# A planned attention and feed-forward kernel: load estimates, mask products, priorities and the last output re-laid

## The chip, the core and the metric

The kernel runs on one NeuronCore of a Trainium2 chip. The metric is the device time of one execution in microseconds (us), lower being better. A core has a matrix engine (TensorE, "PE"), whose products go to PSUM banks; a vector engine (VectorE, "DVE") and a scalar engine (ScalarE, "ACT"), which read PSUM and SBUF; GpSimd ("POOL"), which copies within SBUF and here issues the loads; and SyncE ("SP"), which here issues stores and transposing transfers. Each engine runs its own instructions in order and waits on semaphores for the others.

## The reference

Eight batches of eight heads with 576 tokens and 64 columns go through masked attention; the result is laid out as 4608 tokens of 512 columns and goes through a feed-forward block with a squared relu.

```python
scores = scale * np.matmul(q, k.transpose(0, 1, 3, 2))
mask_local = (rel >= 0) & (rel < stride)                    # stride = 32, heads 0 to 3
mask_strided = (rel >= 0) & (pos[None, :] % stride == pos[:, None] % stride)   # heads 4 to 7
scores = np.where(masks[None, :, :, :], scores, -1000000000.0)
attn = np.exp(scores - np.max(scores, axis=-1, keepdims=True))
attn = attn / (np.sum(attn, axis=-1, keepdims=True) + 1e-09)
x = np.matmul(attn, v)            # then transposed to (4608, 512)
h = x @ w_in                      # (512, 2048)
r = np.maximum(h, 0.0)
g = s * (r * r) + b
out = g @ w_out                   # (2048, 512)
```

## The kernel before

**Attention.** Heads are handled in pairs, four pairs to a batch, called (b, m). Pairs m = 0 and 1 are local: six tiles of 96 queries against 128 keys. Pairs 2 and 3 are strided: eight tiles of 72. A pair (`pair_steps`) transposes q and k, either on PE (`trans`) or from batch 3 to 5 on by a transposing transfer on SP (`k_dma`, `q_dma`); spreads q so that its two heads lie in separate columns (`q_spread`, a copy on ACT, DVE or POOL); forms scores (`score`, L623); takes exponentials on ACT (L641); multiplies by v with a column of ones for the sums (`av`, L684); divides on DVE; and transposes the result into `xT`, on PE or by a transfer. In batch 0 (`b < PE_MASK`) the mask is added in PSUM: each score product of 192 or 144 columns is preceded by a product of the identity with large negative numbers (L620). From batch 1 on the mask is a multiplication on DVE after the exponential.

**Feed-forward.** The 4608 tokens are nine tiles T of 512. `ff1` (L983) multiplies `xT` by `w_in`, ACT or DVE take the relu and the square. T = 0 and 1 go through `ff2` (L1238). From T = 2 on the second product uses seven products P1 to P7 of halves instead of eight (`ff2_seven`, L951), and T = 7 and 8 do the same for the first one (`ff1_seven`, L1208). In the last tile P3 comes last; its 16 products go to two banks, eight for rows t = 0 and eight for t = 1, and each bank is evicted by one `scalar_tensor_tensor` on DVE into a tile "o" and stored by SP (`store`, L882 and L886). The tiles "o" come from a pool of three buffers (`op`), taken in turn; a new one waits until the store of the third one before it has landed.

**The order.** Nothing is ordered by hand on the engines. `lay_out` runs a planner (`class Plan`) in the host's Python that keeps an assumed time `t` of PE and emits, one after another, the steps of attention and feed-forward in the order that all engines then run. PE steps are chosen in the loop at the end: attention if it is behind its due time (`due`, with the constant `ahead`), otherwise feed-forward. Work for the other engines is posted with what it needs and its assumed cost (`post`), and `flush` emits what is ready, the smallest ready time plus a priority first. Priorities by kind of work stand in `ORDER`. `ORDERS` is 0, so the order is taken as it stands.

When data of a load will be there is assumed too: `landing(cost)` keeps a time `ring` at which the stream of loads is through, adds the cost of each load, and adds 0.6 us, or 6 us after 60 us. Transposing transfers ("D", "Y") count as landed 12 us, copies out to DRAM ("X") 7 us after their issue (`LAT`). The loads of batch b + 2 (`fetch_qk`, then `fetch_v`) are posted to POOL when batch b's q and k are through and the k transfers of batch b + 1 are under way; in front of them stand two small copies on POOL (`gate`, L1323) which wait for these transfers. After v has landed, `rows_before` copies its rows by 32 partitions, on ACT or DVE, queued at the planned time of the landing.

At the start PE runs filler products (`keep_running`, L1502) until q and k are there.

Of the kernel before, what the change touches and what calls it, by code (L numbers as in the profile page):

```python
# [18 lines left out]
class Plan:  # L19
# [7 lines left out]
    LAT = {"A": 70.0, "V": 70.0, "P": 70.0, "D": 12000.0, "X": 7000.0, "Y": 12000.0}  # L27

    def __init__(self, order):
        self.t = 0.0  # L30
        self.SLACK, self.ahead, self.LATER = order["SLACK"], order["ahead"], order
        self.done = {}
        self.pend = []
        self.free = {"A": 0.0, "V": 0.0, "P": 7000.0, "D": 0.0, "X": 0.0, "Y": 0.0}
        self.banks = {}

# [7 lines left out]

    def flush(self):
        while True:
            best = None
            for p in self.pend:
                r = self.ready_at(p[0])
                if r is None or r > self.t:  # L50
                    continue
                if p[1].keys() <= {"A", "V"} and min(
                        self.free[e] for e in p[1]) > self.t + self.SLACK:
                    continue
                k = p[3][0]
                w = r + self.LATER.get(k[0] if isinstance(k, tuple) and k[2:3] != (0,) else None, 0.0)
                if best is None or w < best[0]:
                    best = (w, r, p)
            if best is None:
                return  # L60
            _, r, p = best
            self.pend.remove(p)
            eng = min(p[1], key=lambda e: max(self.free[e], r) + p[1][e])
            end = max(self.free[eng], r, self.t - self.SLACK) + p[1][eng]
            self.free[eng] = end
            p[2](eng)
            for k in p[3]:
                if isinstance(k, Group):
                    self.banks[k.name] = end + self.LAT[eng]
                    k = ("rel", k)  # L70
                soon = isinstance(k, tuple) and k[0] == "soon"
                self.done[k] = end + (6000.0 if soon else p[4] or self.LAT[eng])

# [44 lines left out]
class Step:  # L118
    def __init__(self, fn, ns, needs=(), group=None, keys=(), posts=(), after=None):
# [4 lines left out]
ORDER = {"g": 1500.0, "S": 2500.0, "in": 2500.0, "w_mix": 0.0, "wc": 1000.0, "ev": 1000.0,  # L124
         "c21": 1500.0, "c11": 500.0, "c12": 500.0, "C22": -1500.0, "fv": 0.0, "Vb": -400.0,
         "x": -1500.0, "Ub": 1000.0, "xc": -1500.0, "fe": -400.0, "k": 1500.0, "fu": -1500.0,
         "Va": 500.0, "p": 0.0, "c22": 500.0, "Ua": 2500.0, "e": -1500.0, "q": 0.0, "r": 0.0,
         "u": 0.0, "SLACK": 600.0, "ahead": 0.05}
KINDS = ("g", "S", "in", "w_mix", "wc", "Va", "Ua", "Ub", "Vb", "C22", "xc", "q", "k", "r", "x", "e",
         "p", "u", "ev", "fv", "fu", "fe", "c11", "c22", "c21", "c12")  # L130


def varied(order, rnd):

    order = dict(order)
    for kind in rnd.sample(KINDS, rnd.choice((1, 2, 4))):
        order[kind] = rnd.choice((-1500.0, -800.0, -400.0, 0.0, 500.0, 1000.0, 1500.0, 2500.0))
    if rnd.random() < 0.2:
        order["SLACK"] = rnd.choice((400.0, 600.0, 800.0, 1000.0))
    if rnd.random() < 0.2:  # L140
        order["ahead"] = rnd.choice((0.0, 0.05, 0.1, 0.2))
    return order
# [46 lines left out]
def lay_out(ctx, tc, nc, q, k, v, moe_w_in, moe_w_out, moe_s, moe_b, out, order, q_shape, out_shape,  # L189
# [284 lines left out]
    def pair_steps(b, m):  # L474
# [135 lines left out]
        def score(i, group):  # L610
# [3 lines left out]
            def f():  # L614
                if i % per_s == 0:
                    st["s", g] = bank(group)
                c = i % per_s * 2 * nq
                if b < PE_MASK:

                    nc.tensor.matmul(  # L620
                        out=st["s", g][0:nk, c:c + 2 * nq], lhsT=ident[0:nk, 0:nk],
                        rhs=neg_loc if loc else neg_str, start=True, stop=False)
                nc.tensor.matmul(  # L623
                    out=st["s", g][0:nk, c:c + 2 * nq], lhsT=(st["k"][:, i * nq:i * nq + nk] if loc else st["k"][:, i, 0:SQ]),
                    rhs=st["q"][:, i].rearrange("d e c -> d (e c)"), start=b >= PE_MASK, stop=True)

            s = Step(f, (2 if b < PE_MASK else 1) * (2 * nq / 2.4 + 8), needs=[("q", id_), ("k", id_)],
                     group=group if i % per_s == 0 else None)
# [30 lines left out]

        gr = None  # L660
        for i in range(nt):
            if i % per_s == 0:
                gr = group_of("s", b, m)
            steps.append(score(i, gr))
# [188 lines left out]
    def ff2_seven(T):  # L853
# [24 lines left out]
        def store(i, k, of, plus, ts=slice(0, 2)):  # L878
            def g(eng):
# [3 lines left out]
                    out=o[:, ts], in0=src, scalar=s_sb[:, 0:1],  # L883
                    in1=plus()[:, ts], op0=ALU.mult, op1=ALU.add)
# [3 lines left out]
                        "(t p) m -> p t m", p=128)[:, ts], in_=o[:, ts])  # L888
# [51 lines left out]
        for key, group, name, fresh, lhs, rhs, needs, more, posts in seq:  # L940
            for t in range(2):
                for k in range(H):
                    halves = last and name == "W"

                    def f(k=k, t=t, group=group, name=name, fresh=fresh, lhs=lhs, rhs=rhs, key=key,
# [3 lines left out]
                        elif fresh and t == k == 0:  # L949
                            gts[name, T] = bank(group).rearrange("p (t m) -> p t m", t=2)  # L950
                        nc.tensor.matmul(out=gts[name, T, t][:, 0] if halves else gts[name, T][:, t],  # L951
                                         lhsT=lhs(k, t), rhs=rhs(k),
                                         start=fresh and k == 0 and (halves or t == 0),
                                         stop=t == 1 and k == H - 1, skip_group_check=True)
                    s = Step(f, 110, needs=needs(k) + ([(x[0], T, t) if halves and x == d("C22")
# [3 lines left out]
                    if k == H - 1 and key == "P3" and last:  # L959
                        s.keys = [("P3", T, t)]  # L960
                        s.posts = [([("P3", T, t)], {"V": 420.0},
                                    store(0, 1, "W", val("Ub"), slice(t, t + 1)),
                                    [Ws[t]])]
# [3 lines left out]
                    if t == 1 and k == H - 1 and key == "P3":  # L967
# [338 lines left out]
    ring = 0.0  # L1306
    LONG_V = 4

    def landing(cost):

        nonlocal ring
        ring = max(ring, plan.t + 2000.0) + cost

        return ring + (6000.0 if plan.t > 60000.0 else 600.0)
# [4 lines left out]
    def fetch_qk(b):  # L1319
# [6 lines left out]
        for name in ("q", "k"):  # L1326
            if b >= (QB_DMA if name == "q" else KB_DMA):
                arrive(both(name + "l", b), landing(4600))
                continue
            if b < HEAD_T:  # L1330
                arrive(both(name + "l", b), landing(2400 if name == "q" else 2600))
                continue
            plan.done["raw", name, b] = landing(1700 if b > 1 else 2400 if name == "q" else 2500)
            for mm in range(2):
                pair_post(b, name, mm, ("raw", name, b))
        for name in ("qs", "ks"):
            arrive(both(name, b), landing(2000 if b > 1 else 1200))

    def fetch_v(b):
        load_vl(b)  # L1340
        plan.done["raw", "vl", b] = landing(4600)
# [4 lines left out]
        else:  # L1346
            load_vs(b)
            arrive(both("vs", b), landing(5000))

    def early_v(b):  # L1350
# [3 lines left out]
        plan.done["raw", "v", False, b] = landing(1800 if b > 1 else 1300)  # L1354
# [27 lines left out]
    plan.done["sb_row",] = 16000.0  # L1382
    def weights_in(eng):

        nonlocal ring
        nc.gpsimd.tensor_copy(out=gate[0:8, 2:3], in_=loaded[0, "qs"][64:SQ, 0:1])
        load_w_in()
        ring = 13200.0
        for keys, cost in ([0], 2700), ([1], 2500), ([2], 2500), ([3], 2500):
            arrive([("w_in", c) for c in keys], landing(cost))  # L1390
# [7 lines left out]
    def weights_out(chunks):  # L1398
        load_w_out(chunks)
        for c in chunks:  # L1400
            arrive([("w_out", c)], landing(2400 if c < 3 else 3000))

    def second(eng):
# [5 lines left out]
        plan.done["raw", "vl", 1] = landing(2600)  # L1409
# [16 lines left out]
    for b in range(B):  # L1426
        for m in range(4):
            steps, last_av = pair_steps(b, m)
            att.append(steps)
            if b + 2 < B:  # L1430

                if m == 0:
                    plan.post(
                        [("fetch_v", b + 1) if b else ("free",)] +
                        [("q", (b, mk)) for mk in range(4)] + [("k", (b, mk)) for mk in range(4)] +
# [79 lines left out]
    def due():  # L1515

        pos = f1_pos[i1] + (f2[i2 - 1].pos if i2 else 0.0) + plan.ahead
        return (pos if pos <= 1 else 1 + (pos - 1) / 2) * batch_ns

    while i2 < len(f2) or any(at_i[p] < len(att[p]) for p in range(len(att))):  # L1520
# [17 lines left out]
        if len(order) == 2 and i1 % 4 == 0 and f1_pos[i1] > (f2[i2 - 1].pos if i2 else 0.0) + 1:  # L1538
# [57 lines left out]
```

## Time and profile before

| | |
|---|---|
| median of 3 runs | 298.2 us (298.0 to 298.53) |
| the profiled execution | 298.86 us |
| its span, first to last instruction | 297.1 us |
| PE matmuls | 2802 |
| DVE, ACT, POOL instructions | 501, 336, 140 |
| first products on real data (L494) | 5.33 us |
| first feed-forward product (L983) | 18.96 us |
| last eviction on DVE begins | 293.61 us |
| stores to the output, median from issue to landing | 2.9 us (256 KB) |

The profile has for every instruction its engine, its start and its duration, the line of the kernel that issued it, and the names of the tiles that it writes and reads (out<-in). From the semaphores it also has what ended each idle stretch of an engine. The duration of a product includes its way through the array, so products overlap: those of 512 columns last 379 ns and start about 213 to 216 ns apart. The share of DMA is that of the 16 engines that move the data. "L951" is line 951 of the kernel.

### The profile page before, as it was taken

How to read it: one execution, taken by the hardware profiler on the slowest of the kernel's cores; microseconds unless marked ns; L12 is line 12 of the kernel's file. 1: busy time of each engine (PE TensorE's matmuls, PEld its weight loads, DVE VectorE, ACT ScalarE, POOL GpSimd, SP SyncE). 2: the span in 40 equal slices, each digit the busy share in tenths (PEclk: the TensorE clock that was granted, in tenths of full speed). 3: DMA queues.
4: the chain of work that ended last, by engine and by line, in shares of the span. 5: the costliest groups of instructions: out<-in, count | busy, mean ns of one | idle time of the engine just before them, and what ended most of it. 6: DMA issues, size and time to landing. Idle time of an engine off the chain costs nothing.

```text
span 297.1 us, 7092 instructions
## 1 busy us (share of the span) xinstructions
PE 290.5 (98%) x2802; PEld 220.0 (74%) x2802; DVE 235.3 (79%) x501; ACT 194.3 (65%) x336; POOL 93.7 (32%) x140
## 2 busy tenths in 40 slices
PE   8999999999999999999999999999999999999995
PEld 3775656666556568889767776768888989999984
DVE  5857888798966988787877896759898588888963
ACT  3577957898838798647774878469877545675400
POOL 8873624601980296009710394100000000000000
PEclk9999999999999999999999999999999999999999
DMA  8999999997999499989999999999230300110214
GB/s 136 189 206 203 218 180 184 223 171 119 109 195 149 67 132 138 170 173 122 148 136 144 182 170 105 143 140 207 44 97 0 108 29 9 71 38 3 95 48 142
DMA packets 106152, 38.19 MB, mean 129 GB/s; under 512 B 85414, under 2 KB 103974, under 8 KB 106118
## 3 DMA queue, kind: packets, MB, share of 16 engines
q0 software_dynamic: 60848, 18.23, 62.7%
q1 hardware_dynamic: 45270, 19.51, 36.0%
q8 instruction: 22, 0.36, 0.5%
q14 instruction: 12, 0.10, 0.1%
HBM read 36.99 MB, written 10.62 MB: 160 GB/s over the span
## 4 chain that ended last, share of the span: by engine, by line
PE 88%; DMA 6%; ACT 2%; DVE 2%; POOL 1%; issue 1%; ACTq 0%
PE ps_f L983 28%; PE ps_f L951 22%; PE ps_f L1238 8%; DMA v_loc<-in_v_dram 6%; PE ps_s L623 5%; PE ps_f L1208 3%; PE ps_a L684 3%; PE ps_s L1502 2%; PE ps_a L1208 2%; PE ps_s L951 2%; PE ps_t L1208 2%; PE ps_s L1208 2%; PE ps_t L951 1%; PE ps_s L1238 1%; PE ps_t L684 1%; PE ps_t L502 1%
## 5 line engine op out<-in xcount | busy, mean ns | idle before, releaser
L983 PE MATMUL ps_f<-xT,w_in_sb 128*128 128x512 f16 (+4 forms) x568 | 115.5, 331 | 0.3 <-ACT u L1009 0.3
L1009 ACT ACTIVATE u<-ps_f 128x512 f16<-128x512 f32 x104 | 61.0, 594 | 32.5 <-PE ps_f L983 31.8
L983 PEld LDWEIGHTS <-w_in_sb 128*128 128x128 f16 x576 | 57.4, 114 | 23.2 <-issue 0.5
L951 PEld LDWEIGHTS <-gT 128*128 128x128 f16 x608 | 58.4, 98 | 9.2
L951 PE MATMUL ps_f<-w_out_sb,gT 128*128 128x256 f16 x376 | 55.6, 273 | 0.0
L1017 ACT ACTIVATE gT<-u 128x1024 f16<-128x1024 f16 x29 | 30.7, 1057 | 0.8
L1238 PE MATMUL ps_f<-w_out_sb,gT 128*128 128x512 f16 x112 | 30.4, 379 | 0.0
L951 PE MATMUL ps_f<-w_mix,gT 128*128 128x256 f16 x176 | 25.1, 273 | 0.0
L641 ACT ACTIVATE p_str<-ps_s 72x432 f16<-72x432 f32 (+1 forms) x46 | 20.7, 482 | 6.4 <-PE ps_s L623 5.8
L711 DVE TENSOR_TENSOR x_nat<-ps_a,rec 96x384 f16<-96x384 f32 (+2 forms) x46 | 24.1, 523 | 0.6
L641 ACT ACTIVATE p_loc<-ps_s 128x384 f16<-128x384 f32 x46 | 21.4, 494 | 4.8 <-PE ps_s L623 4.3
L1019 DVE TENSOR_TENSOR gT<-u 128x1024 f16<-128x1024 f16 x27 | 18.5, 686 | 5.9 <-ACT u L1009 5.4
L819 DVE TENSOR_TENSOR gT<-gT 128x1024 f16<-128x1024 f16 x34 | 22.4, 678 | 0.6 <-ACT gT L1017 0.4
L382 POOL DMA_DIRECT2D v_loc<-in_v_dram x24 | 17.7, 757 | 8.6 <-DMA w_out_sb<-in_moe_w_out_dram 5.7
L951 PEld LDWEIGHTS <-S 128*128 128x128 f16 x176 | 17.1, 98 | 2.9
L1238 PEld LDWEIGHTS <-gT 128*128 128x128 f16 x128 | 11.4, 98 | 7.8
L387 POOL DMA_DIRECT2D v_str<-in_v_dram x16 | 13.0, 816 | 12.3 <-PE ps_f L983 3.6
L684 PEld LDWEIGHTS <-p_str 72*128 72x128 f16 x256 | 12.8, 98 | 5.1 <-ACT p_str L641 0.4
L1323 POOL COPY gate<-kT 1x1 f16<-1x1 f16 x6 | 1.5, 256 | 45.0 <-DMA kT<-ks 45.0
L951 PE MATMUL ps_f<-w_mix,S 128*128 128x256 f16 x112 | 15.5, 273 | 0.0
L701 DVE RECIPROCAL rec<-ps_a 96x6 f32<-96x6 f32 (+2 forms) x47 | 8.6, 182 | 8.6 <-PE ps_a L684 8.4
L1149 ACT ACTIVATE gT<-u 128x1024 f16<-128x1024 f16 x12 | 12.7, 1058 | 1.7 <-DVE u L1128 1.4
(237 smaller groups left out, 529.7 us busy)
## 6 DMA issues: line engine op xcount, KB each, us to landing
out_dram<-o SPq DMA_DIRECT2D x34, 256.0 KB, 2.9
w_in_sb<-in_moe_w_in_dram POOLq DMA_DIRECT2D x4, 512.0 KB, 9.7
w_out_sb<-in_moe_w_out_dram POOLq DMA_DIRECT2D x4, 512.0 KB, 9.9
qs<-in_q_dram POOLq DMA_DIRECT2D x6, 288.0 KB, 8.4
ks<-in_k_dram POOLq DMA_DIRECT2D x6, 288.0 KB, 9.7
v_loc<-in_v_dram POOLq DMA_DIRECT2D x24, 72.0 KB, 9.6
ql<-in_q_dram POOLq DMA_DIRECT2D x4, 288.0 KB, 9.0
kl<-in_k_dram POOLq DMA_DIRECT2D x16, 72.0 KB, 3.6
```

Of the source, the lines that this page charges most:

```text
L382: nc.gpsimd.dma_start(out=vl[LPAD:128, h, :, 0:D], in_=v_band(b, h))
L641: nc.scalar.activation(out=st["pw", g][0:nk, 0:2 * n * nq], in_=st["s", g][0:nk, 0:2 * n * nq], func=AF.Exp, scale=scale)
L684: nc.tensor.matmul(out=st["pa", g][:, n % 6, :], lhsT=st["pw", gp_][0:nk, i * nq:i * nq + WIDE], rhs=vt[0:nk, 2 * mm + e, j, :])
L711: nc.vector.tensor_tensor(out=x_at(0, cnt), in0=st["pa", g][0:nq, 0:cnt, 0:D], in1=st["rec", g][0:nq, 0:cnt].to_broadcast([nq, cnt, D]), o ...
L819: {"V": nc.vector, "P": nc.gpsimd}[eng].tensor_tensor(out=at(out), in0=at(x), in1=at(y), op=op)
L951: nc.tensor.matmul(out=gts[name, T, t][:, 0] if halves else gts[name, T][:, t], lhsT=lhs(k, t), rhs=rhs(k), start=fresh and k == 0 and (ha ...
L983: nc.tensor.matmul(out=gts["h", T, ft][:, lo:hi], lhsT=w_in_sb[ft // 4][:, ct].rearrange("p (x l) -> p l x", l=4)[:, ft % 4], rhs=xT[ct][: ...
L1009: nc.scalar.activation(out=u, in_=gts["h", T, ft], func=AF.Relu)
L1017: nc.scalar.activation(out=g, in_=u, func=AF.Square)
L1019: nc.vector.tensor_tensor(out=g, in0=u, in1=u, op=ALU.mult)
L1208: nc.tensor.matmul(out=st[bk][:, 256 * t:256 * t + 256], lhsT=lhs(t, c), rhs=rhs(c), start=fresh and t == c == 0, stop=t == c == 1, skip_g ...
L1238: nc.tensor.matmul(out=gts[id_], lhsT=gts[T][:, ft, ts * 128:(ts + 1) * 128], rhs=w_out_sb[:, ft, cols], start=(ft == 0), stop=(ft == NFT ...
```

## The change

The planner gets a new account of transfers. `landing` becomes a method with smaller costs (ql or kl by transfer 4.6 to 2.4 us, v_loc 4.6 to 2.7, v_str 5.0 to 3.3, qs and ks 2.0 to 1.6) and adds 0.7 us at all times (v_str 1.2). Each transfer that SP issues for the plan ("D", "X", "Y") puts 1 us on every load that is under way (`shared`). `LAT` for transposing transfers goes from 12 to 10 us, and to 7 when no load is under way. `fetch_qk` needs q's transposing transfer instead of its spread copy. Priorities can be given to single pieces of batch 0 (`late`), `ahead` gets an addition by stage, and the threshold that puts the second feed-forward product first becomes `lead`; all numbers of `ORDER` are new. In batch 0 one mask product covers all score products of a bank (`forbid`), needs only the constants, and takes the bank. In the last tile, P3's products for t = 1 are done in two halves of 128 columns, each evicted and stored by itself.

```diff
-    LAT = {"A": 70.0, "V": 70.0, "P": 70.0, "D": 12000.0, "X": 7000.0, "Y": 12000.0}
+    LAT = {"A": 70.0, "V": 70.0, "P": 70.0, "D": 10000.0, "X": 7000.0, "Y": 10000.0}
...
+    def landing(self, cost, keys, wait=700.0):
+
+        self.ring = max(self.ring, self.t + 2000.0) + cost
+        for k in keys:
+            self.done[k] = self.ring + wait
+        self.loads.append(keys)
+
+    def shared(self, cost=1000.0):
+
+        self.loads = [x for x in self.loads if self.done[x[0]] > self.t + 1000.0]
+        for x in self.loads:
+            for k in x:
+                self.done[k] += cost
+        if self.ring > self.t:
+            self.ring += cost
...
+    def late(self, k):
+
+        if not isinstance(k, tuple):
+            return 0.0
+        at = k[1] if len(k) > 1 and isinstance(k[1], tuple) else k[2:4] if k[0] == "in" else ()
+        if len(at) == 2 and at[0] == 0:
+            own = k[0] + (k[1] if k[0] == "in" else "") + "0" + str(at[1])
+            if own in self.LATER:
+                return self.LATER[own]
+        return 0.0 if k[2:3] == (0,) else self.LATER.get(k[0], 0.0)
...
-                w = r + self.LATER.get(k[0] if isinstance(k, tuple) and k[2:3] != (0,) else None, 0.0)
...
+                    w = r + self.late(p[3][0])
...
             p[2](eng)
+            if eng in "DXY":
+                self.shared()
...
-                self.done[k] = end + (6000.0 if soon else p[4] or self.LAT[eng])
+                self.done[k] = end + (6000.0 if soon else p[4] or self.LAT[eng] - (
+                    3000.0 if eng in "DY" and self.ring < self.t else 0.0))
...
-         "u": 0.0, "SLACK": 600.0, "ahead": 0.05}
...
+         "ahead3": 0.0, "q00": 1500.0, "SLACK": 800.0, "ahead": 0.2}
...
-                if b < PE_MASK:
-
-                    nc.tensor.matmul(
-                        out=st["s", g][0:nk, c:c + 2 * nq], lhsT=ident[0:nk, 0:nk],
-                        rhs=neg_loc if loc else neg_str, start=True, stop=False)
...
+        def forbid(i, group):
+
+            n = min(per_s, nt - i)
+
+            def f():
+                st["s", i // per_s] = bank(group)
+                nc.tensor.matmul(
+                    out=bank(group)[0:nk, 0:2 * n * nq], lhsT=ident[0:nk, 0:nk],
+                    rhs=(neg_loc if loc else neg_str)[:, None, :].to_broadcast([nk, n, 2 * nq]),
+                    start=True, stop=False, skip_group_check=True)
+            return Step(f, 2 * n * nq / 2.4 + 3, needs=[("negs",)], group=group)
...
+                if b < PE_MASK:
+                    steps.append(forbid(i, gr))
             steps.append(score(i, gr))
...
-        def store(i, k, of, plus, ts=slice(0, 2)):
+        def store(i, k, of, plus, ts=slice(0, 2), ms=slice(0, 256)):
             def g(eng):
                 o = op.tile([128, 2, 256], FP32, tag="o", name="o")
...
+            ends = [(t, k, slice(0, 256)) for t in range(2) for k in range(H)]
+            if last and key == "P3":
+                ends = ends[0:H] + [(1, k, slice(128 * c, 128 * c + 128)) for c in range(2)
+                                    for k in range(H)]
...
-                        s.keys = [("P3", T, t)]
-                        s.posts = [([("P3", T, t)], {"V": 420.0},
-                                    store(0, 1, "W", val("Ub"), slice(t, t + 1)),
-                                    [Ws[t]])]
+                        s.keys = [("P3", T, t, ms.stop)]
+                        s.posts = [([("P3", T, t, ms.stop)],
+                                    {"V": 480.0 if ms.stop - ms.start == 256 else 280.0},
+                                    store(0, 1, "W", val("Ub"), slice(t, t + 1), ms),
+                                    [Ws[t]] if ms.stop == 256 else [("P3", T)])]
...
-        return ring + (6000.0 if plan.t > 60000.0 else 600.0)
...
-                arrive(both(name + "l", b), landing(4600))
+                plan.landing(2400, both(name + "l", b))
...
-            arrive(both(name, b), landing(2000 if b > 1 else 1200))
+            plan.landing(1600 if b > 1 else 1200, both(name, b))
...
-        plan.done["raw", "vl", b] = landing(4600)
+        plan.landing(2700, [("raw", "vl", b)])
...
-            arrive(both("vs", b), landing(5000))
+            plan.landing(3300, both("vs", b), 1200)
...
-                        [("q", (b, mk)) for mk in range(4)] + [("k", (b, mk)) for mk in range(4)] +
+                        [("qT" if b >= (QB_DMA if mk < 2 else QS_DMA) else "q", (b, mk))
+                         for mk in range(4)] + [("k", (b, mk)) for mk in range(4)] +
...
+        pos += order_.get(f"ahead{int(pos / 3)}", 0.0)
...
-        if len(order) == 2 and i1 % 4 == 0 and f1_pos[i1] > (f2[i2 - 1].pos if i2 else 0.0) + 1:
+        if len(order) == 2 and i1 % 4 == 0 and f1_pos[i1] > (f2[i2 - 1].pos if i2 else 0.0) + lead:
```

## The prediction

> **What bounds the kernel now.** I read the page first (busy shares, slices, queues), then the waits of each engine, then busy time by stretch, then the chain of waits and the timeline at the places where TensorE (PE) is not full.
>
> ```profile
> PE 290.5 (98%) x2802; PEld 220.0 (74%) x2802; DVE 235.3 (79%) x501; ACT 194.3 (65%) x336; POOL 93.7 (32%) x140
> ...
> DMA  8999999997999499989999999999230300110214
> ...
> q0 software_dynamic: 60848, 18.23, 62.7%
> q1 hardware_dynamic: 45270, 19.51, 36.0%
> ```
>
> PE is full. The DMA engines are full too, until slice 27 (about 207 us): the loads that POOL issues (q0) and the transposing transfers that SP issues (q1) share them. Where PE has room shows in stretches (length, then PE, its weight loads, DVE, ACT, POOL, clock, DMA share, GB/s):
>
> ```profile
> 10.00:20.00 10.00, 9.13 (x174) 7.93 (x173) 7.58 (x25) 7.16 (x24) 9.31 (x16) 1.00 1.35 196
> 20.00:30.00 10.00, 9.87 (x85) 5.23 (x82) 6.40 (x11) 7.97 (x15) 3.43 (x7) 1.00 1.27 204
> 30.00:180.00 150.00, 150.00 (x1439) 104.36 (x1434) 123.51 (x271) 110.57 (x197) 68.82 (x98) 1.00 1.35 155
> 180.00:200.00 20.00, 19.65 (x149) 13.62 (x148) 13.28 (x27) 12.05 (x19) 3.27 (x4) 1.00 1.65 138
> 200.00:220.00 20.00, 19.58 (x229) 16.66 (x228) 18.20 (x44) 17.41 (x30) 0.00 (x0) 1.00 0.57 112
> 220.00:240.00 20.00, 19.76 (x182) 17.74 (x180) 15.17 (x32) 12.20 (x19) 0.00 (x0) 1.00 0.19 61
> ```
>
> From 30 to 180 us PE never rests. From 20 to 240 us it rests 0.13 + 0.35 + 0.42 + 0.24 = 1.1 us; a better order of the middle can win no more than that. The rest is the head (0.87 us idle in the second row, with filler and small products around it) and the tail after the last product. One wait in the middle has a name, on the waits and on the chain:
>
> ```profile
> ACT v_loc L404 <- DMA v_loc<-in_v_dram: 3.3, 2, 2.5
> ...
> 178.55 16.76 DMA v_loc<-in_v_dram
> ...
> 195.51 0.51 issue
> 196.02 0.59 ACT u L1009
> ```
>
> ACT stood 2.5 us in front of a copy of rows of v that hadn't landed, and the relu eviction queued behind it held PE. At the end, DVE:
>
> ```profile
> 291.87 0.75 DVE L882 SCALAR_TENSOR_TENSOR o<-ps_f,sb_all,Ua 128x512 f32<-128x512 f32 x1 [1.00 <-PE ps_f L951]
> 292.74 0.48 DVE L882 SCALAR_TENSOR_TENSOR o<-ps_a,sb_all,Ub 128x256 f32<-128x256 f32 x1
> 293.61 0.48 DVE L882 SCALAR_TENSOR_TENSOR o<-ps_f,sb_all,Ub 128x256 f32<-128x256 f32 x1 [0.39 <-PE ps_f L951]
> ```
>
> The last eviction ends at 294.09 us; its transfer is issued at 294.11 and its landing signal comes at 296.16 (records of landings); 0.92 us later the span ends.
>
> **What the Trainium skill says.** Page "DMA: Bandwidth & Descriptors", section "Issuing engines are not separate DMA queues": transfers issued from SP and from GpSimd run on the same 16 engines and interleave. The trace agrees: 62.7% and 36.0% add to 98.7%, and a v_loc load took 4.8 to 5.2 us to land for batch 4, but 12.4 to 16.8 us for batch 7. Same page, "Anatomy of one DMA": a transfer carries about 2.0 us that don't depend on its size, most of it completion. Here a 256 KB store took 2.57 us and 128 KB stores 1.74 to 2.05. Page "PSUM — Partial Sum Buffer", "PSUM bank collisions raise a hardware error": a bank that PE writes must not be read at that moment, columns apart or not. No wait in this trace shows it, since each bank here is filled and then read. Same page, "Engine vs sequencer instructions": ACT and DVE queues are strict FIFO; the 2.5 us above show it.
>
> **The change, part by part.** All against the profiled execution: 298.86 us, of which the span is 297.1; the median of the runs is 298.2, 0.66 lower.
>
> 1. *Last output in column halves.* The last 8 products of P3 (t = 1; 256 columns, 0.109 us apart: 0.87 / 8) become 16 of 128 columns. Nearest row: 12 products of 65 columns took 0.55 us with a 0.19 us tail, 33 ns each, so weight loads don't bind at that width and 128 columns cost 53 to 57 ns: 16 x 55 = 0.88 us, nothing lost. The skill's 81 ns ("TensorE: Matmul & The Clock Gate", "Back-to-back issue gap") would make it 1.3 us. The eviction shrinks: 0.745 us at 512 columns and 0.48 at 256 give 0.35 at 128, so 0.13 saved, and half a transfer, about 0.19 (256 KB of packets ran for 1.0 us, a fourth of that is 0.25; 128 KB ran near 0.4). If nothing else happened the tail would gain up to 0.3 us. But each store takes a new tile "o" from a pool of three. The order is C22 twice, P2, P4, P3 (t = 0), P3 (t = 1). Today the last store reuses P2's tile: that transfer landed at 293.11, and a DVE queue entry at 293.1 is that wait, over before the product was done. With a seventh store, the last reuses P4's tile. P4 is evicted 291.87 to 292.62, its 256 KB transfer is issued at 292.64 and lands at 295.21. So the last half can be evicted from 295.21 + 0.05, ends at 295.61, is issued at 295.63 and lands 1.56 later (1.75 of an undisturbed 128 KB store, less 0.19): 297.19 against 296.16, **+1.0 us**. Bounds: +0.8 (fifteen of P4's sixteen signals were there at 294.98) to +1.3 (512-byte rows slower than 1 KB ones). Behind the waiting eviction there is only its store, and for that the end of the kernel waits. The bank rule adds a wait beneath: the first half is planned in 200 ns after its last product, about four products into the second half, and PE's last four may wait for its read (0.35 us). The longer wait covers it; without the pool wait it would still cost about 0.2.
>
> 2. *Mask products a bank wide.* Batch 0 has 28 mask products (12 of 192 columns, 16 of 144). They become 12, with the same columns: 12 x 80 + 16 x 60 ns = 1.9 us either way; sixteen issues go, at some 4 ns (mask and score together run at 165 ns for 160 ns of columns): 0.06 us. What matters is the place: a mask no longer waits for q and k. Only the first of each three can move ahead, as the next two wait for a bank; at about 0.16 us each, four pairs hoist 0.6 us into time where PE ran filler or waited for evictions. Of it, what lies before the first weights (w_in's first chunk lands at 17.10) only moves slack. The cost side: a bank is held longer while s and f1 are short.
>
> 3. *New order numbers in the head.* From 17.10 to 21.3 PE ran six feed-forward products (6 x 0.213 = 1.3 us); the other 2.9 us went to the rest of batch 0's attention, with 0.9 us idle or lost. That is the ceiling. Which of these priorities acts can't be read off by hand; for parts 2 and 3 I take **-0.4 us**, bounds -1.8 and +0.6.
>
> 4. *Loads and transfers in one stream.* From the fetch of a batch to the landing of the last v_loc load, the old sum is 2.0 + 4.6 + 4.6 + 2.0 + 2.0 + 4.6 + 6.0 = 25.8 us; the new one 2.0 + 2.4 + 2.4 + 1.6 + 1.6 + 2.7 + 0.7 = 13.4, plus 1.0 for each SP transfer while the load counts as under way. The trace has 17.8 (batch 5: 102.30 to 120.07), 24.5 (batch 6) and 26.2 (batch 7). With SP's transfers at their times in the trace I count 2, 2 and 8 of them: 15.4, 15.4, 21.4. So the new sum is 2.4, 9.1 and 4.8 us short for v_loc. For q and k it is nearer than the old one (batch 6's ql: 5.1 new, 12.6 old, 5.3 in the trace). The row copies of v that today stood 2.4 to 3.2 us after the planned landing are put on ACT or DVE by that sum. With the 2.5 us that their priority adds, and transfers that move forward and count more, batch 6's copy comes 2 to 4 us ahead of its data and batch 7's 2 to 3, as now. The 2.5 us of today cost PE about 0.35 us at the gap and part of the 0.42 behind it; a second such block is worth the same or a little more, as two feed-forward banks hold about 0.9 to 1.7 us of work: **+0.8 us**, bounds -0.7 (no block, and most of today's rests gone) and +4.
>
> 5. *Fetch held for q's transfer and not for its spread copy; shorter transfer latency (12 to 10 us).* POOL waits 11 to 16 us per batch in front of its gate on the next batch's k transfer (45.0 us over six waits): that is next in line, so an earlier fetch costs and gains nothing. Transfers took 3.0 to 10.4 us where a landing shows; 10 us plus issue still covers them. Nothing.
>
> Sum: +1.0 - 0.4 + 0.8 = +1.4 us: 300.3 for the profiled execution, **299.6** against the median.
>
> **Rivals.**
> - *Tail and row copies as above*: 299.6, own range 298.9 to 300.9. For it: the rotation of three is visible in today's waits. Against: the middle is estimated.
> - *The head pays* (the other side): the new order brings batch 0's attention forward into the time before 17.10 us. Price: at most 2.9 us; at -1.5 there, -0.9 in the middle and +1.0 at the end it gives 296.8. It decides once head and middle together save over 1.6 us. For it: 0.9 us plainly lost there, and the new sums fit the loads of batches 1 to 3 (batch 3's last load of v: 66.7 us in the trace, 67.1 when the costs are summed from the weights on). Against: batch 0's chain runs through ACT and DVE, which no edit shortens.
> - *Even*: head and middle save about 1.0 us and the tail takes it: 298.2.
> - *ACT and DVE become the bound around 150 and 190 us*: copies stand 5 us ahead of their data in both batches, PE loses 5 - 1.7 = 3.3 us in one and 0.5 in the other: 298.2 + 1.0 - 0.4 + 3.3 + 0.5 = 302.6.
> - *The halves don't part*: the second half is only ready after the first is read, so the split never saves; within the first case.
>
> **How the numbers follow.** Chances 0.47, 0.26, 0.16 and 0.11. A measurement of this kernel can tell about 0.2%, 0.6 us, from no change: faster 0.26, same 0.16, slower 0.47 + 0.11 = 0.58. The range runs from 297.0 to 301.8: it leaves out about one in ten on each side, and holds the bounds of the tail, of the head and of one long block.
>
> **What would show it.** Tail: DVE's last eviction 128 wide, about 0.35 us, with some 1.2 us of idle time before it put down to out_dram's transfer, and PE's last product as now. Wrong if that eviction starts within 0.3 us of PE's end. Middle: ACT or DVE waits for v_loc over 2 us near batches 6 and 7, PE rests of more than 1.1 us between 30 and 240 us. Head: PE gapless before 21.0 us. If PE's last product ends over 1.6 us sooner than 293.4, the second case holds.

## The result, and the profile after

| | before | after |
|---|---|---|
| median of the runs | 298.19 us (298.0 to 298.53) | 310.56 us (309.19 to 316.43) |
| profiled execution | 298.86 us | 310.45 us |
| its span | 297.1 us | 308.6 us |

The ratio is 1.040, interval 1.036 to 1.043: 12 us slower, where 299.6 was forecast and 301.8 was the top of the range. Medians and ranges in this document are of all executions of a kernel, while ratios leave out those that lie over 1.5% above the kernel's fastest. The changed code has other line numbers: L983 is now L1046 (ff1), L951 L1014 (ff2_seven), L404 L452 (the copies), L882 L940 (the last evictions), L1009 L1072 (relu).

Section 1 of the page after, its two slice rows for PE and DMA, and its queues:

```profile
PE 291.3 (94%) x2794; PEld 218.5 (71%) x2794; DVE 234.5 (76%) x489; ACT 194.4 (63%) x335; POOL 99.9 (32%) x148
...
PE   7999999999999899699799998799999999999993
...
DMA  8999999998999999999999999933610200110213
...
q0 software_dynamic: 60848, 18.23, 62.8%
q1 hardware_dynamic: 45414, 19.51, 39.2%
```

PE is busy for the same time within 0.8 us. The span grew by rests, and they lie in slices 14 to 26 of 40. Stretches of the middle (length, then PE, weight loads, DVE, ACT, POOL, clock, DMA share, GB/s), after:

```profile
100.00:120.00 20.00, 18.57 (x173) 12.00 (x171) 16.01 (x37) 15.50 (x27) 14.81 (x23) 1.00 1.71 131
120.00:140.00 20.00, 16.92 (x203) 15.04 (x202) 14.92 (x32) 14.18 (x27) 9.77 (x14) 1.00 1.46 136
140.00:160.00 20.00, 18.09 (x162) 14.42 (x161) 12.03 (x26) 12.36 (x21) 7.99 (x11) 1.00 1.77 142
...
180.00:200.00 20.00, 17.49 (x136) 12.27 (x134) 12.64 (x22) 12.75 (x23) 4.33 (x6) 1.00 1.67 159
```

From 100 to 202 us PE rests 9.5 us in eight places, where before it rested 0.8 in two. The waits of the engines after (waiting line, releaser: total, times, longest):

```profile
POOL qD_str L452 <- DMA qT<-qs: 20.9, 2, 13.0
...
ACT qD_str L452 <- DMA qT<-qs: 8.8, 3, 3.8
...
ACT qD_loc L452 <- DMA qTl<-ql: 2.9, 2, 2.0
...
DVE x_nat L769 <- DMA xT<-x_nat: 2.2, 2, 1.4
...
PE ps_f L1046 <- DMA xT<-x_dram: 1.9, 1, 1.9
...
ACT v_loc L452 <- DMA v_loc<-in_v_dram: 1.5, 1, 1.5
```

In this list the copies on ACT, DVE and POOL wait for a *transposing transfer* far more than for rows of v. SP, which issues these transfers, stood for the loads that they read (SP's own waits after):

```profile
SPq L622 <- DMA ql<-in_q_dram: 14.2, 6, 5.8
...
SPq L603 <- DMA kl<-in_k_dram: 6.3, 4, 2.8
...
SPq L630 <- DMA qs<-in_q_dram: 2.7, 2, 1.5
```

Before, SP shows no such waits from 90 to 205 us: in batches 5 to 7 each transfer of q or k was issued at least 3.9 us after its load had landed. One case in full. The chain of waits after has (start, length)

```profile
117.00 10.92 DMA qT<-qs
```

and ACT's timeline after (in brackets the idle time before, and what ended it)

```profile
128.00 1.36 ACT L452 COPY qD_str<-qT 64x576 f16<-64x576 f16 x2 [3.82 <-DMA qT<-qs]
129.39 0.60 ACT L1072 ACTIVATE u<-ps_f 128x512 f16<-128x512 f32 x1
129.88 0.87 ACT L685 ACTIVATE p_loc<-ps_s 128x384 f16<-128x384 f32 x2
```

and PE's timeline after

```profile
130.42 0.33 PE L666 MATMUL ps_s<-qD_loc,kT_alt 128*128 128x192 f16 x2 [1.74 <-ACT p_loc L685]
```

SP issued the transfer of q at 117.00, when its load of qs had just landed (116.87, 14.4 us after the fetch began); it landed 10.9 us later. ACT came to the copy that spreads q at 124.18 and stood. Behind it stood a relu and two exponentials; PE rested until the first exponential had given back its bank.

How late the stream of loads was is in the list of issues. Batch 5's loads went out from 102.43 on. By the new account (2.0 + 2.4 + 2.4 + 1.6 + 1.6 + 2.7 + 3.3 us, 1.2 for v_str, and 1 us for each of the eight transfers that SP issued meanwhile) v_str is there by about 127.6; the last of it landed at 130.88. By the old account (2.0 + 4.6 + 4.6 + 2.0 + 2.0 + 4.6 + 5.0, and 6) it is 133.2. SP's transfers are issued earlier as well: batch 7's first transfer of q went out at 172.91, before at 179.77. That the 10.9 us come from sharing the engines with the loads is likely, but no run shows it by itself.

To compare kernels I add up PE's *lost pace*: the time from one product's start to the next, less columns / 2.4 ns. (It falls below 0 where narrow products start closer than that, as those of L1265 in the kernel before.) In us, by stretch of the profiled execution:

```
                            0-22  22-60  60-100  100-205  205-280  280-end   span
before                       5.8   -0.8     1.1      4.1      2.3      0.3   297.1
after                        5.8   -0.4     1.2     13.7      1.8      2.3   308.6
e7  halves alone             5.8   -0.8     1.1      3.1      2.2      0.9   297.6
e8  masks alone              5.4   -0.1     2.0      3.9      3.2      0.4   300.7
e10 priorities alone         6.1   -1.0     1.1      4.4      3.2      0.3   298.3
e13 account alone            6.1   -0.8     2.8     13.2      2.3      0.6   308.2
e17 account, pad 3 us        6.0   -0.8     2.4      7.4      2.2      0.4   302.4
e14 account, pad 6 us        5.8   -0.8     1.6      3.8     10.3      0.5   305.3
e15 e14 without counting     6.3   -0.5     3.3     14.3      2.1      0.6   310.2
e18 before, pad 4.5 us       6.2   -0.8     1.1      4.8      2.9      0.4   299.2
e5  before, pad 0.6 us       5.9   -0.8     1.1     18.5      3.7      0.7   313.7
e6  after, pad 6 us          5.7   -0.4     1.1      3.8      7.2      1.8   305.0
```

Of the 11.5 us between before and after, 9.6 lie between 100 and 205 us and 2.0 at the end.

The tail, on the timeline after 301.7 us:

```profile
302.44 0.83 PE L1014 MATMUL ps_f<-w_out_sb,S 128*128 128x128 f16 x12
302.54 3.47 SPq L944 DMA_DIRECT2D out_dram<-o  x4
303.84 0.48 DVE L940 SCALAR_TENSOR_TENSOR o<-ps_a,sb_all,Ub 128x256 f32<-128x256 f32 x1 [1.32 <-DMA out_dram<-o]
304.47 0.35 DVE L940 SCALAR_TENSOR_TENSOR o<-ps_f,sb_all,Ub 128x128 f32<-128x128 f32 x1
304.88 0.38 PE L1014 MATMUL ps_f<-w_out_sb,S 128*128 128x128 f16 x4 [1.61 <-DVE o L940]
...
305.30 0.35 DVE L940 SCALAR_TENSOR_TENSOR o<-ps_f,sb_all,Ub 128x128 f32<-128x128 f32 x1 [0.47 <-PE ps_f L1014]
```

The 128-wide evictions of 0.35 us and a wait for a buffer are there, but the wait stands one eviction earlier than forecast, and PE's last four products wait 1.61 us until DVE has read the first half.

### The profile page after: what moved, and what is told of

The parts are those of the page before. It is cut to its first block, busy times and chain, and to the rows that moved or that the text cites. A ratio compares the mean times of both kernels' runs of the same rounds, so it can differ in the third digit from the quotient of the medians.

```text
span 308.6 us, 7069 instructions
## 1 busy us (share of the span) xinstructions
PE 291.3 (94%) x2794; PEld 218.5 (71%) x2794; DVE 234.5 (76%) x489; ACT 194.4 (63%) x335; POOL 99.9 (32%) x148
## 4 chain that ended last, share of the span: by engine, by line
PE 71%; DMA 19%; POOL 4%; issue 2%; ACT 2%; DVE 1%; DVEq 0%; POOLq 0%; ACTq 0%
PE ps_f L1046 22%; PE ps_f L1014 17%; PE ps_f L1301 7%; DMA xT<-x_dram 4%; PE ps_s L666 4%; DMA qT<-qs 4%; DMA v_str<-in_v_dram 3%; DMA ks<-in_k_dram 3%; PE ps_f L1271 3%; DMA xT<-x_nat 2%; PE ps_a L742 2%; PE ps_a L1271 2%; PE ps_t L1271 2%; PE ps_s L1271 2%; PE ps_s L1014 2%
## 5 line engine op out<-in xcount | busy, mean ns | idle before, releaser
L1046 PE MATMUL ps_f<-xT,w_in_sb 128*128 128x512 f16 (+4 forms) x568 | 119.0, 331 | 3.9 <-ACT u L1072 2.0
L1072 ACT ACTIVATE u<-ps_f 128x512 f16<-128x512 f32 x105 | 61.8, 597 | 31.5 <-PE ps_f L1046 30.1
L1046 PEld LDWEIGHTS <-w_in_sb 128*128 128x128 f16 x576 | 57.3, 114 | 25.1 <-issue 4.5
L1014 PEld LDWEIGHTS <-gT 128*128 128x128 f16 x608 | 58.5, 98 | 9.6
L1014 PE MATMUL ps_f<-w_out_sb,gT 128*128 128x256 f16 x376 | 52.8, 273 | 0.0
L1082 DVE TENSOR_TENSOR gT<-u 128x1024 f16<-128x1024 f16 x28 | 19.2, 687 | 20.0 <-ACT u L1072 19.6
L1080 ACT ACTIVATE gT<-u 128x1024 f16<-128x1024 f16 x28 | 29.6, 1058 | 0.7
L1014 PE MATMUL ps_f<-w_mix,gT 128*128 128x256 f16 x176 | 25.6, 272 | 0.0
L877 DVE TENSOR_TENSOR gT<-gT 128x1024 f16<-128x1024 f16 x34 | 24.2, 734 | 0.3 <-ACT gT L1212 0.3
L769 DVE TENSOR_TENSOR x_nat<-ps_a,rec 96x384 f16<-96x384 f32 (+2 forms) x45 | 23.1, 514 | 1.4 <-DMA xT<-x_nat 0.7
L1014 PEld LDWEIGHTS <-S 128*128 128x128 f16 x184 | 17.0, 98 | 4.0 <-issue 1.7
L742 PEld LDWEIGHTS <-p_str 72*128 72x128 f16 x256 | 14.5, 98 | 5.1 <-issue 0.9
L452 POOL COPY qD_str<-qT 64x576 f16<-64x576 f16 x8 | 6.3, 792 | 35.4 <-DMA qT<-qs 20.9
L1014 PE MATMUL ps_f<-w_mix,S 128*128 128x256 f16 x112 | 16.0, 273 | 0.0
L877 DVE TENSOR_TENSOR S<-gT 128x1024 f16<-128x1024 f16 x18 | 12.3, 681 | 2.9 <-PE ps_f L1014 2.3
```

Of the source, the lines that this page charges most:

```text
L742: nc.tensor.matmul(out=st["pa", g][:, n % 6, :], lhsT=st["pw", gp_][0:nk, i * nq:i * nq + WIDE], rhs=vt[0:nk, 2 * mm + e, j, :])
L769: nc.vector.tensor_tensor(out=x_at(0, cnt), in0=st["pa", g][0:nq, 0:cnt, 0:D], in1=st["rec", g][0:nq, 0:cnt].to_broadcast([nq, cnt, D]), o ...
L877: {"V": nc.vector, "P": nc.gpsimd}[eng].tensor_tensor(out=at(out), in0=at(x), in1=at(y), op=op)
L1014: nc.tensor.matmul(out=dst[:, ms], lhsT=lhs(k, t), rhs=rhs(k)[:, ms], start=fresh and k == 0 and (halves or t == 0), stop=t == 1 and k == ...
L1046: nc.tensor.matmul(out=gts["h", T, ft][:, lo:hi], lhsT=w_in_sb[ft // 4][:, ct].rearrange("p (x l) -> p l x", l=4)[:, ft % 4], rhs=xT[ct][: ...
L1072: nc.scalar.activation(out=u, in_=gts["h", T, ft], func=AF.Relu)
```

## The experiments

Theory A: the planner calls loads landed too early; copies and transposes then stand in ACT's, DVE's, POOL's and SP's queues ahead of their data, and PE runs dry. Rivals: the new priorities, the shorter transfer latency, or the new mask products do it.

**e1.** The changed kernel with the whole old account (old costs and pad, no `shared`, latency 12).

```diff
-            self.done[k] = self.ring + wait
+            self.done[k] = self.ring + (6000.0 if self.t > 60000.0 else 600.0)
...
-                self.shared()
```

> The changed kernel with the old account of transfers (old load costs, 6 us added after 60 us, transposing transfers at 12 us, nothing put on loads by SP's transfers); new priorities, masks, halves stay. Theory A (copies on ACT, DVE and POOL stand ahead of data that the new account calls landed too early): the rests of PE between 100 and 202 us fall from 9.5 to under 2.5 us, time 300 to 303 us. Rival B (the new priorities pull attention ahead of its data): rests stay above 6 us, time 307 us or more. Rival C (the DMA engines themselves became slower): rests stay, and loads of batch 7 still take as long as now.

308.94 us (305.7 to 313.79), ratio 1.026 (1.024 to 1.028). The profiled execution is the one of 305.7, 4.7 us under after, with 5.2 us of lost pace in the middle instead of 13.7. The account is a cause, but the other parts together cost about 7 us without it (305.7 against 298.9).

**e2.** The changed kernel with the old numbers of `ORDER`.

> The changed kernel with the old numbers of ORDER (priorities, SLACK, ahead 0.05, lead 1). Theory A: the new account still calls data landed too early, rests of PE between 100 and 202 us stay above 5 us, time 305 to 312 us. Rival B: they fall under 2.5 us, time 299.5 to 302 us.

311.88 us, ratio 1.043 (1.041 to 1.046). The priorities aren't the cause in the middle.

**e3 and e4.** The changed kernel with latency 12 and nothing taken off; and with only the 3000 not taken off.

```diff
-                self.done[k] = end + (6000.0 if soon else p[4] or self.LAT[eng] - (
-                    3000.0 if eng in "DY" and self.ring < self.t else 0.0))
+                self.done[k] = end + (6000.0 if soon else p[4] or self.LAT[eng])
```

> The changed kernel with transposing transfers counted as landed 12 us after their issue at all times, as before the change, load costs new. If within theory A the transfers' part decides: ACT and POOL no longer stop in front of q's spread copies, rests of PE between 100 and 202 us fall from 9.5 to about 3 us, time 302 to 304 us. If the loads' part decides: above 307 us.

> The changed kernel with only the shortening to 7 us taken out (transposing transfers count as landed after 10 us at all times). If that shortening is what puts the spread copies 3 to 4 us early: 303 to 306 us. If 10 us is itself too short against the 10.2 to 10.9 us that the trace shows: above 307 us.

e3 314.94 us, 1.055 (1.051 to 1.060); e4 307.9 us (305.72 to 312.02), 1.030 (1.024 to 1.037), with the middle at 9.3 in an execution of 305.7. Against the whole change e4 gains about 3 us by the ratios (their intervals just touch): counting transfers as landed after 7 us costs something. A longer latency alone doesn't repair it: in e3 PE waited 7.3 us for transfers of k, and copies still waited for transfers of q.

**e5.** The kernel before with one constant changed.

```diff
-        return ring + (6000.0 if plan.t > 60000.0 else 600.0)
+        return ring + 600.0
```

> The kernel before with one constant changed: loads after 60 us count as landed 0.6 us instead of 6 us after their place in the stream. Nothing else of the change. Theory A (loads called landed too early): PE rests between 100 and 205 us grow from 0.8 us by several us, time 302 us or more. If theory A is wrong and the slowdown comes from the latency of the transposing transfers, the fetch or the priorities: 297.5 to 299.5 us.

314.87 us, ratio 1.053 (1.050 to 1.057): 16.6 us for a constant. Its waits:

```profile
ACT v_loc L404 <- DMA v_loc<-in_v_dram: 17.4, 5, 5.7
...
PE ps_f L983 <- ACT u L1009: 8.7, 3, 5.0
```

Here it is rows of v, as the prediction had feared; a relu behind them holds PE.

**e6.** The changed kernel with the 6 us put back after 60 us.

> The changed kernel with the 6 us put back on loads after 60 us, all else of the change kept (small costs, 1 us for each SP transfer, 10 or 7 us for transposing transfers, new priorities). Theory A: the middle loses 2 us or less against before, time 300 to 303 us. If the sum of the costs is too short by more than 6 us or the transfers' part decides: above 305 us.

306.9 us, ratio 1.027 (1.023 to 1.032). The middle is repaired (3.8 of lost pace, as before); from 205 to 280 it loses 7.2 instead.

**e9.** e5, but v_loc keeps 5.4 us of the pad.

> As e5 (the kernel before with 0.6 us instead of 6 us on loads after 60 us), but the v_loc load, which the row copies on ACT and DVE wait for, keeps its 6 us. If the row copies standing on ACT and DVE ahead of their load make e5's loss: most of the 16.6 us goes, time 298.5 to 304 us, and no stop of ACT or DVE on v_loc over 2.5 us. If q and k by transfer decide as much: above 308 us.

309.87 us, ratio 1.037 (1.031 to 1.043). Against e5 5 us are back, a third. PE now stopped for transfers of k (L623, twice 1.3 us), but its longest stop, 2.5 us, still came from rows of v, though their load had kept its pad. DVE stood in front of their copy, with the mask multiplications that PE needs behind it (waits of e9):

```profile
DVE v_loc L404 <- DMA v_loc<-in_v_dram: 8.3, 4, 4.7
...
PE ps_t L684 <- DVE p_loc L649: 2.5, 1, 2.5
```

So e9 doesn't part the cost of v from that of q and k.

**e7 and e12.** The halves of the last output alone; the same with four buffers "o".

```diff
-    op = ctx.enter_context(tc.tile_pool(name="op", bufs=3))
+    op = ctx.enter_context(tc.tile_pool(name="op", bufs=4))
```

> The kernel before with only the last output in column halves. The wait on the third store before: +1.0 us by the prediction's sum, up to +1.6 with PE waiting for the read of the first half; time 299.2 to 299.9 us. If it gains: 297.9 to 298.1 us.

> The kernel before with the last output in halves, as e7, and four buffers for output tiles. By the tail's working the wait for P4's store (1.6 us in e7) goes, and what is left is PE's wait for the read of the first half (about 0.4 us), the smaller eviction and store (0.3 us): 298.0 to 298.6 us. If the halves cost by something else than the buffer: 299.3 us or more.

e7 299.61 us, ratio 1.0055 (1.0034 to 1.0075), which is +1.3 us on its 298.31. The timeline of its tail:

```profile
291.60 3.42 SPq L886 DMA_DIRECT2D out_dram<-o  x4
...
292.37 0.35 DVE L882 SCALAR_TENSOR_TENSOR o<-ps_f,sb_all,Ub 128x128 f32<-128x128 f32 x1 [0.19 <-PE ps_f L956]
292.77 0.38 PE L956 MATMUL ps_f<-w_out_sb,S 128*128 128x128 f16 x4 [0.44 <-DVE o L882]
...
294.31 0.35 DVE L882 SCALAR_TENSOR_TENSOR o<-ps_f,sb_all,Ub 128x128 f32<-128x128 f32 x1 [1.59 <-DMA out_dram<-o]
```

P4's store is issued at 291.60 and lands 2.59 us later; only then can the last half be evicted. It lands at 296.25, 4.65 us after P4's issue, before 3.52. With a fourth buffer it is 3.59, and the time 298.66 against 298.86, ratio 0.999 (0.997 to 1.001): the wait is gone, and no gain is left.

**e8 and e11.** The mask products a bank wide alone; the same with four buffers "o".

> The kernel before with only the mask products a bank wide. By the prediction between -0.4 and +0.3 us: 297.8 to 298.5 us; PE work up to 22 us shows 16 issues fewer. The planner lays the head anew, so an order that meets a wait there would show as rests of PE before 22 us.

> The kernel of e8 (only the mask products changed) with four instead of three buffers for output tiles; the order of all engines is that of e8. In e8 P4's eviction stood 2.55 us before a store whose sixteenth signal came 2 us after its fifteenth, while a 16 KB instruction fetch ran on one of the engines. If that wait makes most of e8's +4.1 us: 299.5 to 301 us, wait gone. If the head's masks make it: 302 to 303 us.

e8 302.45 us, ratio 1.012 (1.010 to 1.015), 4.1 us. The head gains 0.4 us; the planner, fed other costs at the start, moves some 350 of PE's 2802 products to other places in the order. Lost pace is 0.7 to 0.9 higher in each of three later stretches, and P4's eviction stood 2.55 us for a buffer. e11: 303.19 us (301.46 to 307.91). In the profiled execution (305.24) the buffer wait was down to 0.34 us, but ACT stood 5.8 us at 198 us for rows of v and PE 3.7 behind it. With such scatter e11 decides nothing on the buffer's worth.

**e10.** The priorities, `late`, `lead` and the additions to `ahead` alone, in the kernel before.

> The kernel before with only the new numbers of ORDER, the priorities of single pieces of batch 0, the stages of ahead and lead 0.9. If the new numbers, found for the new account, cost by themselves: 301 us or more, with rests where a copy on POOL, ACT or DVE waits for a transfer. If they are neutral: 297.5 to 299.5 us. If the head gains: below 297.5 us, PE gapless before 21 us.

300.32 us, ratio 1.0051 (1.0032 to 1.0069): +1.5 us.

**e16.** One edit in the kernel before: the fetch waits for qT and not for the spread copy.

> The kernel before with one edit: the fetch of q and k waits for the transposing transfer's landing (qT) of the late batches instead of the spread copies. Theory A: loads start a little earlier into the same stream, and with the pad in force nothing is late: 298 to 299.5. Rival: the earlier loads slow the transposing transfers and hold up the spread copies: 300 to 303.

298.74 against 298.65 us, ratio 0.999 (0.997 to 1.001): nothing. The traces say why: every engine has the same instructions in the same order as before, so on the old plan the edit moves nothing. What it does within the new account wasn't tried alone.

**e13.** All of the account, and nothing else, in the kernel before.

```diff
+            self.done[k] = self.ring + wait
...
+                self.shared()
...
-                arrive(both(name + "l", b), landing(4600))
+                plan.landing(2400, both(name + "l", b))
```

> The kernel before with all of the change's account of loads and transfers (landing, shared, the lower load costs, 10000 instead of 12000, the 3000 taken off, the fetch that waits for qT), and with the old priorities, the old mask products and the old last output. Theory A (loads are called landed too early, and in-order queues stand ahead of their data): this part alone costs most of the loss, 305 to 312, with the lost pace of TensorE between 100 and 205 us at 9 to 18 us and the idle time of TensorE there ended by copies of q, k or v that waited for transfers. Rival B (the account is harmless on the old plan, and only together with the re-laid head it hurts): 298 to 301.

312.51 us (309.98 to 316.47), ratio 1.036 (1.027 to 1.046); span 308.2 against 308.6 of the whole change, the middle 13.2 against 13.7. PE's timeline:

```profile
147.22 0.38 PE L1015 MATMUL ps_f<-xT,w_in_sb 128*128 128x512 f16 x1
152.16 0.82 PE L655 MATMUL ps_s<-qD_loc,kT_loc 128*128 128x192 f16 x4 [4.56 <-DMA kT_loc<-kl]
```

and SP's timeline has the transfer:

```profile
142.28 5.46 SPq L587 DMA_TRANSPOSE kT_loc<-kl  x2
```

PE's scores stand in front of a k that landed at 152.11, 9.8 us after its issue; the last rows of v of that fetch landed at 160.53. One stop of 4.6 us is half of the middle's extra loss. The transfer kept within the 10 us that the account allows; it was issued too late for PE's place in the order.

**e14, e17, e15.** e13 with a pad of 6 us after 60 us; with 3 us; and with 6 us but without counting the transfers.

> The account alone, with 6000 in place of the wait of 700 after 60 us. Theory A: the pad repairs it, 298 to 301.5, lost pace between 100 and 205 us 3 to 6 us. If the lower load costs and the later transfers matter by themselves: 302 to 307. Below 297.6 it would beat the kernel before, which the counting of transfers alone would then be worth.

> The account alone with 3000 after 60 us, between e13 (700: the middle lost 13.2 us, attention's last transfer at 218.5) and e14 (6000: the middle lost 3.8, but attention's last transfer came at 235.6 and PE ran out of feed-forward work). If the two costs trade against each other step by step: middle 5 to 9 us, last transfer of xT before 226, no rest of 4 us near 240, and 300 to 305 in all. If the pad must be whole to cover the transfers: 308 or more with q, k or v waits as in e13. If any pad delays attention: a rest at 230 to 240 as in e14.

> The account with the pad of 6000, and without the 1 us that each spread copy's transfer adds to the loads under way. If the counting protects the plan by itself: 2 us or more above e14. If the pad already covers it, as theory A has it: within 1.5 us of e14.

e14 306.95 us (306.26 to 307.32), ratio 1.026 (1.019 to 1.032); e17 305.51 (302.45 to 309.63), 1.019 (1.011 to 1.027); e15 311.09 (308.62 to 312.01), 1.037 (1.028 to 1.046). The pad trades: with 0.7, 3 and 6 us the middle loses 13.2, 7.4 and 3.8, and attention's last transfer of x is issued at 218.5, 224.3 and 235.6 us (before: 219.8). In e14 PE's next products then need sums on DVE (`qD_loc`) that read this x, and PE stands (PE's timeline in e14):

```profile
234.24 0.27 PE L1240 MATMUL ps_s<-qD_loc,ks 128*128 128x256 f16 x1
239.05 0.80 PE L1240 MATMUL ps_s<-qD_loc,ks 128*128 128x256 f16 x3 [4.54 <-DVE qD_loc L1115]
```

That is e6's loss after 205 us too (its last transfer: 235.2). Without the counting, e15's ACT stood in front of rows of v (its timeline):

```profile
152.65 0.73 ACT L434 COPY v_loc<-v_loc 32x640 f16<-32x640 f16 x1 [7.08 <-DMA v_loc<-in_v_dram]
157.45 0.73 ACT L434 COPY v_loc<-v_loc 32x640 f16<-32x640 f16 x1 [4.07 <-DMA v_loc<-in_v_dram]
158.08 1.06 ACT L1039 ACTIVATE u<-ps_f 128x512 f16<-128x512 f32 x2
```

and PE 8.5 us behind it. So with the lower costs the counting does protect the rows of v; what it adds is too little without a pad, and with the pad of 6 it comes on top.

**e18.** The kernel before with a pad of 4.5 us.

> The kernel before with 4500 in place of 6000. If the pad of 6000 is only just long enough (theory A, with loads up to 16.8 us late in its trace): 301 to 307, with v_loc waits of 2 us and more in front of ACT or DVE. If it has slack: 297.5 to 299, and below 297.6 a version that beats both kernels.

302.3 us (300.52 to 304.69), ratio 1.014 (1.006 to 1.022); ACT stood 4.2 us for rows of v. The old account has not even 1.5 us to give. None of the eighteen kernels beat the one before beyond its interval.

## Why the prediction was wrong, point by point

- *Part 1, the tail* (+1.0): right. The mechanism is e7's timeline, the size +1.1 from P4's issue to the last landing, +1.3 on the median. In the whole change the "0.35 us" of PE's wait for the read became 1.61, since a store of Vb signalled late (below) and DVE read the first half late. One reading was off without bearing on the sum: of the 128 KB stores before, given as 1.74 to 2.05 us, the one issued at 293.47 took 2.38.
- *Parts 2 and 3, the head* (-0.4): wrong sign. The head itself is even (5.8 and 5.8). Masks alone cost 4.1 us and priorities 1.5. I priced the edits where they stand; they go into a planner, and everything after them is laid out anew.
- *Part 4* ("+0.8 us, bounds -0.7 and +4"): **this is the step that failed.** The account alone costs 11 us of span (e13). The sums for v were right ("2.4, 9.1 and 4.8 us short for v_loc"); what was made of them was not. "For q and k it is nearer than the old one" was checked on ql alone. For ks the same sum gives 10.7 us from the start of the fetch in batch 6 and 13.7 in batch 7, and the trace before has 16.0 and 18.1. And PE's loss was held to one more block like the one in the trace, "worth the same or a little more", in front of rows of v. But the account dates q's and k's loads, transfers and copies too: SP stood 14.2 us for ql in after, copies on ACT and DVE stood behind late transfers, and each blocked copy holds a relu or an exponential, and so PE. PE itself stood 4.6 us for k in e13.
- *Part 5* ("10 us plus issue still covers them. Nothing."): wrong too, but the smaller part. Where a landing shows, transfers took 3.0 to 10.4 us before. Issued 8 to 11 us earlier, q's in after took 10.9 and k's in e13 9.8. That the change counts some of them at 7 us the prediction doesn't price; it costs about 3 us (e4). The first half, the fetch that waits for qT, is nothing on the old plan, where it moves no instruction (e16).
- *Rival "ACT and DVE become the bound"* had the kind of failure right, copies ahead of their data, but at 302.6 us it was worth a third of what came.
- By the ratios the account alone costs 10.8 us, masks 3.7, priorities 1.5 and halves 1.6, together more than the 11.9 of the whole. They overlap, and the sum of single parts proves nothing here. What e13 shows is that the account is enough by itself. That it is not all shows in e1, which keeps 305.7 to 313.8 without it.

Open stays how the loss in the whole change divides between q, k and v: e5 stops at v, e13 at k, after at q and x. Also why the re-laid kernels scatter by up to 8 us between executions, when the one before stays mostly within 2.

## What to carry to other kernels

When a planner lays out in-order queues, the pad on an assumed landing is a stall budget: look at the actual landing of *everything* dated by it, and count what stands behind the first late copy, not only the copy. Price such an edit by running it alone, one constant at a time: 4.5 us instead of 6 cost 3.9 us here, 0.6 cost 16.6. And a pad isn't free either: it moves a chain later, and the place to look is where other work for PE runs out.

## What the hardware showed that I had not expected

**A rest costs twice.** The clock granted to PE fell to half after rests: for 3.4 us in e13 (after 4.6 us), 6.8 in e14 (4.5 us) and 10.2 in e15 (8.5 us), always whole steps of 3.4 us. Between 2.2 and 2.5 us both happened: in e3 a rest of 2.26 us was followed by 3.4 us at half clock, one of 2.45 us was not. The Trainium skill, "TensorE: Matmul & The Clock Gate", "Part 1: The HAM clock gate", gives a window of 3.4 us and half the clock after an idle window; the steps agree, but a rest of a whole 3.4 us was not needed here. In after the rests of the middle were 0.3 to 1.9 us and the clock stayed.

**128 columns don't wait for weights.** Twelve products of 128 columns, each with a weight load of its own, took 0.83 us, the last of them 0.22 long: (0.83 - 0.22) / 11 = 55 ns from start to start. The same page has both 81 ns for a stream with weight loads ("Back-to-back issue gap") and 55.6 ns ("Wait — 56ns, not 53.3ns?"); here it was the second.

**A store's last signal can come 2 us late.** In after a 128 KB store issued at 299.84 had fifteen of its sixteen signals at 301.62 and the last at 303.72. A packet of 16 KB of the instruction queue, 1.1 us long, started on one DMA engine at 301.41; near the end there is one every 13 to 15 us. In eight of the twenty traces such a packet starts between issue and landing of one of the last stores, and in each of them a last signal came 1.6 to 2.2 us after the fifteenth. In the other twelve it starts ahead of these stores, and none came over 0.7 us after. The eight are just the kernels with the new mask products, so the packet isn't parted from what else that edit does; that it is the cause wasn't tried.
